# Attention and SwiGLU on one core: batches 4 to 7 with the key decay folded into V and eight heads scored in one run

## The chip, the cores and the metric

The kernel runs on one core of a Trainium2 chip. The metric is the device time in microseconds of one execution. The kernel before took 363.72 us, the median of three runs (363.65 to 364.18).

Engines are named as in the profile: PE (TensorE matmul), PEld (its weight load), DVE (VectorE), ACT (ScalarE), POOL (GpSimd), SP (SyncE, used here as a DMA queue).

## The reference

Eight batches of eight heads, 576 positions, 64 dimensions a head. Causal attention with a decay: `cum` is the running sum of max(s, 0) along the sequence, and a score gets `cum[key] - cum[query]` added before the softmax. The 4608 rows of 512 then go through RMS norm and a SwiGLU layer with 1536 hidden units.

```
scores = scale * q @ k^T                     # scale = 1/8
bias   = -(cum[query] - cum[key])
scores = where(causal, -1e9, scores + min(bias, 0))
attn   = exp(scores - max) ; attn /= sum(attn) + 1e-9
x      = attn @ v                            # [8*576, 512]
xn     = x / sqrt(mean(x*x) + 1e-6) * rms_g
out    = (silu(xn @ w_gate) * (xn @ w_val)) @ w_out
```

The factor exp(-cum[query]) is the same for all keys of a query, so it falls out in the division. What stays is exp(cum[key]), a factor of each key and head. It can be added inside the exponential as a bias of each partition (keys lie on partitions there), or be multiplied into the rows of V and into a column of ones beside V, which gives the sum for the division.

## The kernel before, in words

**Tiles.** A batch's 576 positions are five blocks: four of 128 and a half block of 64. Scores are made transposed, keys on partitions and queries along the free dimension. A step of scores (`s_step`) takes one key block `kb` and half of the heads (`g`), and scores that block's queries and the next block's (256 columns) for four heads. Two heads share PE, one on rows 0 to 63 and one on rows 64 to 127 (`par`), and write to two PSUM banks (`psS`). The half block's step takes all eight heads with 64 columns each. That makes nine steps a batch. Queries further than the next block are not scored: the decay makes them negligible, and a flag worked out on the chip leads to a general path if that does not hold.

ACT takes the exponential head by head, with the head's column of `biasK` as the bias (L302); POOL sets the part above the diagonal to zero (L311). The result lies in one of eight slots of the buffer `E`. An AV step (`av_step`, L344 and L350) multiplies E by V for one query block and four heads: eight matmuls of 65 columns, four for the first block. Its result lies in the bank `psAV` for the first half of the heads and in `psT` for the second. DVE takes the reciprocal of the 65th column (L357) and scales (L359). When both halves are there, ACT sums the squares (L366), POOL works out the norm's factor alpha (L379, L382), DVE scales the row (L389), and a transposing DMA on SP (L400) puts it into `xnT`, a ring of four chunks.

**The FFN.** 512 rows are a chunk; there are nine. `ffn(c)` loops over twelve hidden blocks: four matmuls for the gate (L758), ACT's tanh (L761), four for the value (L767), and DVE's two products U (L770) and Ht (L763). Four row blocks of the output follow, twelve matmuls each (L780), with ACT's copy to `osb` (L785). Gate, value and output take PSUM banks from a ring of four, `psF`.

**The order of the work.** All is written out in one order for each engine when the kernel is built. `step()` is called after every four FFN matmuls: a slot, 36 in a chunk. In each slot a small planner puts in what is ready: pending exponentials and masks, the scale step, loads and casts from side lists (`act_side`, `v_side`, `pool_side`), and in `place()` a score step, an AV step or a transpose. `can_s` and `can_av` hold the rules: so many slots after the inputs were issued, so many since the last step of the kind, and a free slot in E. Score steps come every four slots, nine in 36. `need(c)` puts filler matmuls on PE if a chunk begins before its rows of `xnT` are due; there are none at the starts of chunks now.

**Loads.** For batches 4 to 7, K goes from DRAM to bf16 on the POOL queue (`load_k`), Q comes as fp32 into a raw buffer `kq32` and is cast by POOL (`cast_x`), and both are turned by transposing DMAs on SP (L182). V goes on the POOL queue (`load_v`, L186) into one of two buffers once the AV steps of two batches earlier are done.

## Time and profile before

| | us |
|---|---|
| median of three runs | 363.72 |
| profiled execution, by its span (the page gives no other time of it) | 362.1 |
| PE busy | 346.3 (96%) |
| DVE busy | 275.1 (76%) |
| ACT busy | 240.6 (66%) |
| POOL busy | 174.9 (48%) |
| chunk 0 of the FFN begins, by PE's first gate matmul | 26.5 |
| chunks 3, 4, 5, 6 begin (attention of batches 4 to 7 beside them) | 144.9, 182.6, 220.2, 257.2 |
| chunks 7, 8 begin | 293.3, 324.4 |

The profile is of one execution. In the timeline a row has its start, its length, engine, line, operation and tiles; several equal instructions in a row are merged and counted. PE's lengths overlap, so the distance between starts tells the pace. In the groups by line, "busy, mean ns" comes after the count, then the engine's idle time just before the group and what ended it.

### The profile page before, as it was taken

What the parts mean: (1) busy time and instruction counts of PE and PEld (TensorE: products, weight loads), DVE (VectorE), ACT (ScalarE), POOL (GpSimd) and SP (SyncE); (2) the same over time, 40 slices, a digit from 0 to 9 for tenths busy, and PEclk for the clock granted to TensorE, in tenths of its full rate; (3) what the DMA queues carried; (4) which work ended last, traced back from release to release, by engine and by line L of the source; (5) the groups of instructions that cost most, each with busy time, mean ns of one, the idle gap of its engine ahead of it and who ended that gap; (6) DMA issues with size and microseconds to landing.
All of it is one profiled execution on the core that took longest, in us unless ns stands there. A gap on an engine that the chain in (4) does not pass through costs nothing. (4 is left out here: it accounts for less than half of the span.)

```text
span 362.1 us, 6942 instructions
## 1 busy us (share of the span) xinstructions
PE 346.3 (96%) x2342; PEld 160.6 (44%) x2387; DVE 275.1 (76%) x524; ACT 240.6 (66%) x619; POOL 174.9 (48%) x281
## 2 busy tenths in 40 slices
PE   5889999999999999999999999999999999999993
PEld 2445444543444444444444444444444444444441
DVE  6697988698998889788897988884588558817820
ACT  3988885778787877867778767776777553233311
POOL 6959763738875566979648734622232200000000
PEclk9999999999999999999999999999999999999998
DMA  7999999999999299999999954943200130020011
GB/s 222 144 238 251 173 173 259 170 205 199 172 166 123 31 217 115 181 186 142 184 220 138 128 123 107 128 62 90 71 15 17 60 94 1 0 89 29 1 61 61
DMA packets 124800, 45.68 MB, mean 126 GB/s; under 512 B 103924, under 2 KB 119800, under 8 KB 124760
## 3 DMA queue, kind: packets, MB, share of 16 engines
q0 software_dynamic: 62368, 13.11, 47.6%
q1 hardware_dynamic: 51328, 23.67, 32.5%
q10 hardware_dynamic: 11064, 8.41, 9.5%
q8 instruction: 19, 0.31, 0.4%
q14 instruction: 21, 0.17, 0.2%
HBM read 37.90 MB, written 9.44 MB: 131 GB/s over the span
## 5 line engine op out<-in xcount | busy, mean ns | idle before, releaser
L302 ACT ACTIVATE E<-psS,biasK 128x256 bf16<-128x256 f32 (+3 forms) x328 | 107.3, 413 | 20.5 <-PE psS L278 19.2
L767 PE MATMUL psF<-xnT,wv_sb 128*128 128x512 bf16 x414 | 109.6, 379 | 1.0
L758 PE MATMUL psF<-xnT,wg_sb 128*128 128x512 bf16 x420 | 109.7, 380 | 0.7 <-ACT xnT L416 0.3
L780 PE MATMUL psF<-wout_sb,Ht 128*128 128x512 bf16 x420 | 100.6, 379 | 0.6
L770 DVE SCALAR_TENSOR_TENSOR U<-T,psF 128x512 bf16<-128x512 f32 x108 | 73.7, 682 | 25.5 <-ACT T L761 25.3
L761 ACT ACTIVATE T<-psF 128x512 f32<-128x512 f32 x108 | 64.4, 596 | 41.4 <-PE psF L758 37.5
L311 POOL TENSOR_SCALAR_AFFINE_SELECT E<-E 128x512 bf16<-128x512 bf16 x64 | 45.2, 706 | 84.1 <-ACT E L302 84.1
L763 DVE TENSOR_TENSOR Ht<-U,psF 128x512 bf16<-128x512 bf16 x99 | 67.8, 684 | 7.0
L758 PEld LDWEIGHTS <-wg_sb 128*128 128x128 bf16 x432 | 38.6, 98 | 44.5 <-issue 5.8
L780 PEld LDWEIGHTS <-Ht 128*128 128x128 bf16 x432 | 38.8, 98 | 42.6 <-issue 2.3
L767 PEld LDWEIGHTS <-wv_sb 128*128 128x128 bf16 x432 | 38.5, 98 | 42.2 <-issue 4.0
L785 ACT ACTIVATE osb<-psF 128x512 f32<-128x512 f32 x36 | 21.6, 599 | 33.1 <-PE psF L780 27.6
L389 DVE SCALAR_TENSOR_TENSOR xs_sb<-x_sb,al_all,g_row 128x512 bf16<-128x512 bf16 (+1 forms) x36 | 29.5, 819 | 13.1 <-POOL al_all L382 12.3
L186 POOL DMA_DIRECT2D v_sb<-in_v_dram x40 | 34.8, 872 | 0.0
L366 ACT ACTIVATE xs_sb<-x_sb 128x512 bf16<-128x512 bf16 (+1 forms) x37 | 23.6, 637 | 12.1 <-DVE x_sb L359 11.6
L278 PE MATMUL psS<-kqT 64*128 64x256 bf16 (+2 forms) x304 | 25.9, 256 | 1.6 <-ACT E L302 0.6
L427 DVE TENSOR_TENSOR acc<-acc,mag 128x1280 bf16<-128x1280 bf16 x32 | 27.2, 871 | 0.2
L350 PEld LDWEIGHTS <-E 128*128 128x128 bf16 x320 | 21.7, 98 | 10.1 <-issue 0.2
L382 POOL TENSOR_TENSOR al_all<-al_all,mhalf 128x1 f32<-128x1 f32 (+2 forms) x39 | 22.9, 586 | 3.2
L344 PEld LDWEIGHTS <-E 128*128 128x128 bf16 x256 | 20.0, 98 | 7.7 <-DVE x_sb L359 0.6
L278 PEld LDWEIGHTS <-kqT 64*128 64x128 bf16 x320 | 9.0, 94 | 31.1 <-issue 28.4
L379 POOL TENSOR_SCALAR al_all<-ss_all 128x1 f32<-128x1 f32 (+2 forms) x39 | 9.9, 253 | 25.5 <-ACT xs_sb L366 17.3
(124 smaller groups left out, 301.5 us busy)
## 6 DMA issues: line engine op xcount, KB each, us to landing
out_dram<-osb SPq DMA_DIRECT2D x36, 256.0 KB, 2.3
kq<-in_q_dram ACTq DMA_DIRECT2D x5, 1024.0 KB, 7.8
v_sb<-in_v_dram POOLq DMA_DIRECT2D x32, 128.0 KB, 6.3
kq<-in_k_dram SPq DMA_DIRECT2D x4, 512.0 KB, 5.6
kq<-in_q_dram SPq DMA_DIRECT2D x4, 512.0 KB, 7.5
kq<-in_k_dram ACTq DMA_DIRECT2D x2, 1024.0 KB, 8.8
kqn<-in_k_dram POOLq DMA_DIRECT2D x16, 128.0 KB, 5.6
wout_sb<-in_moe_w_out_dram POOLq DMA_DIRECT2D x2, 768.0 KB, 10.0
```

What stands on the lines that cost most here:

```text
L186: nc.gpsimd.dma_start(out=v_sb[0:n, b % 2, c, :, 0:64], in_=v[b, :, c * 128:c * 128 + n, :].rearrange("h p d -> p h d"))
L278: nc.tensor.matmul(pair[par][:, j * W:j * W + M], lhsT=kT, rhs=qT, start=(j == 0 and not premask), stop=(j == nj - 1))
L302: nc.scalar.activation(out=eo, in_=ei, func=AF.Exp, scale=0.125, bias=biasK[:, kb, bh:bh + 1])
L311: nc.gpsimd.affine_select(out=Ev[:, :, 0:nq], in_=Ev[:, :, 0:nq], pattern=[[0, nh], [1, nq]], compare_op=ALU.is_ge, fill=0.0, base=0, chan ...
L389: nc.vector.scalar_tensor_tensor(out=xs_sb[0:n, (b * NSC + qb) % NX, :], in0=x_sb[0:n, (b * NSC + qb) % NX, :], scalar=al_all[0:n, col:col ...
L427: nc.vector.tensor_tensor(out=acc[:, sl], in0=acc[:, sl], in1=mag[:, sl], op=ALU.max)
L758: nc.tensor.matmul(Gp, lhsT=wg_sb[:, cc, fs], rhs=xnT[:, cc, x0:x0 + DM], start=(cc == 0), stop=(cc == CC - 1))
L761: nc.scalar.activation(out=T, in_=Gp, func=AF.Tanh, scale=0.5)
L763: nc.vector.tensor_tensor(out=Ht[:, fb - 1, :], in0=pend[0], in1=pend[1], op=ALU.mult)
L767: nc.tensor.matmul(Vp, lhsT=wv_sb[:, cc, fs], rhs=xnT[:, cc, x0:x0 + DM], start=(cc == 0), stop=(cc == CC - 1))
L770: nc.vector.scalar_tensor_tensor(out=U, in0=T, scalar=1.0, in1=Gp, op0=ALU.add, op1=ALU.mult)
L780: nc.tensor.matmul(Op, lhsT=Ht[:, fb, tb * 128:(tb + 1) * 128], rhs=wout_sb[:, fb, :], start=(fb == 0), stop=(fb == FB - 1))
```

## The change

Batches 0 to 3 stay. For batches 4 to 7:

- **One run a key block.** `s_run` scores all eight heads at once, into four banks: one from the ring `psF` and `psT` for the second half of the heads, both `psS` banks for the first. Eight matmuls of 256 columns.
- **The half block in the fourth's columns.** The run of block 3 is joined: each head has 128 columns of block 3's own queries, 64 tail queries against block 3's keys, and the same 64 against the half block's keys, in one 256-column field. 24 matmuls. Four runs a batch, not nine steps. In E the half block's scores lie at columns 192 to 255, and the last AV step reads 128 columns from 64 and from 128, so that its 64 rows come out on partitions 64 to 127; the steps behind it work on these (`part_of`).
- **The decay.** `vwx` = exp(biasK) for these batches, once, in chunk 0. `fold_b` on POOL multiplies V's block by it and copies it into the 65th column; an AV step waits for its block's fold.
- **The exponential.** One activation of 512 columns for a bank, without bias: four a run, one in each of the next four slots (`exp_q`).
- **Order.** Runs at least nine slots apart (`PERIOD`). AV steps of these batches use `psAV` for both halves, at least two slots apart. The squares come one slot later and the scale step four slots after its AV.
- **Loads.** Q of these batches alternates between the two raw buffers and is loaded a batch earlier; K and V loads on POOL are two slots apart (`PACE`).

```diff
+    MB = 4
+    PERIOD, PACE = 9, 2
+    vwx = mp.tile([128, NSC, (B - MB) * H], FP32, name="vwx")
+    def raw(b, w):
+        return (b + 1) % 2 if b >= KB else w
...
+    def s_run(b, kb):
+        p, join = b % 2, kb == 3
+        N = 192 if join else 256
+        fb, tt, ps = psF(), psT32(), psS()
+        banks = {1: (fb, tt), 0: (ps[:, 0, :], ps[:, 1, :])}
+        es = {g: take_slot((b, kb, g), 3 if join else 2) for g in (1, 0)}
+        if join:
+            eslot.update({(b, 4, g): es[g] for g in es})
+        def keys(rs, c, hp):
+            return kqTx[rs, p, 0, c, hp, :] if b >= KB else kqTn[rs, p, 0, hp, c * 128:c * 128 + 128]
+        for g in (1, 0):
+            for j in (0, 1):
+                hp = 2 * g + j
+                parts = [(kb, kqTx[:, p, 1, kb:kb + 2, hp, :], 0, 256)]
+                if join:
+                    tail = kqTx[:, p, 1, 4, hp, 0:64].rearrange("d (p r) -> d r p", r=4)
+                    parts = [(3, kqTx[:, p, 1, 3, hp, :].rearrange("d (r p) -> d r p", r=4), 0, 32),
+                             (3, tail, 32, 16), (4, tail, 48, 16)]
+                for i, (c, qT, o, n) in enumerate(parts):
+                    for par in (0, 1):
+                        rs = slice(par * 64, par * 64 + 64)
+                        to = banks[g][par][:, j * 256:j * 256 + 256]
+                        if join:
+                            to = to.rearrange("k (r p) -> k r p", r=4)[:, :, o:o + n]
+                        nc.tensor.matmul(to, lhsT=keys(rs, c, hp), rhs=qT[rs],
+                                         start=(j == 0 and i == 0), stop=(j == 1 and i == len(parts) - 1))
+        def exps(g, par):
+            to = E[:, es[g], 2 * par:2 * par + 2, :]
+            src = banks[g][par]
...
+            nc.scalar.activation(out=to, in_=src, func=AF.Exp, scale=0.125)
+        def mask(g, c, q0, nq):
+            Ev = E[:, es[g], :, q0:q0 + nq]
+            nc.gpsimd.affine_select(
+                out=Ev, in_=Ev, pattern=[[0, 4], [1, nq]], compare_op=ALU.is_ge, fill=0.0, base=0,
+                channel_multiplier=-1)
+            done["S", b, c, g] = slot[0]
+        def part(g, par):
+            exps(g, par)
...
+            if par:
+                pending.append(lambda: mask(g, kb, 0, 128))
+                if join:
+                    pending.append(lambda: mask(g, 4, 192, 64))
...
+        exp_q.extend((join, lambda a=(g, par): part(*a)) for g in (1, 0) for par in (0, 1))
+    def fold_b(b, c):
+        i = (b - MB) * H
+        nc.gpsimd.tensor_tensor(
+            out=v_sb[:, b % 2, c, :, 0:64], in0=v_sb[:, b % 2, c, :, 0:64],
+            in1=vwx[:, c, i:i + H].unsqueeze(2).to_broadcast([128, H, 64]), op=ALU.mult)
+        nc.gpsimd.tensor_copy(out=v_sb[:, b % 2, c, :, 64], in_=vwx[:, c, i:i + H])
+        done["W", b, c] = slot[0]
...
-            ps = psT32() if b > 0 and g == 1 else psAV()
+            ps = psT32() if 0 < b < MB and g == 1 else psAV()
...
+            e, back, own = j, 128, 0
+            if b >= MB:
+                e = 2 * (j % 2) + j // 2
+                if qb == 4:
+                    back, own = 64, 128
...
+        if b >= MB:
+            if slot[0] - last["S"] < 3 or slot[0] - last["run"] < PERIOD or slot[0] - max(last[x] for x in ("AVT", "TT")) < 2:
+                return False
+            return run_ready()
...
-        if b > 1 and not ready(8, "V", b):
+        if b > 1 and not ready(8, "V", b) or b >= MB and not ready(3, "W", b, qb):
...
+        for _ in range(1):
+            if exp_q:
+                exp_q.pop(0)[1]()
...
-            if ready(5 if (b, qb) == (1, 1) else 3, "AV", b, qb, 1):
+            if ready(5 if (b, qb) == (1, 1) else 4 if b >= MB else 3, "AV", b, qb, 1):
...
-            run_side(pool_side)
+            if not run_side(pool_side) and fold_seq and ready(9, "V", *fold_seq[0]):
+                fold_b(*fold_seq.pop(0))
...
+        put(act_side, 30, lambda: nc.scalar.activation(out=vwx, in_=biasK[:, :, MB * H:BH], func=AF.Exp))
```

More of the change, by code (lines that the diff above doesn't have):

```diff
@@ L240, in take_slot, with slot_free @@
         return sl
-    def slot_free():
-        return eread.get(ecount[0] % NE, 0) == 0
+    def slot_free(n=1):
+        return all(eread.get((ecount[0] + i) % NE, 0) == 0 for i in range(n))
     def masks(pair):
@@ L448 @@
     x_seq = []
+    fold_seq = [(b, c) for b in range(MB, B) for c in range(NSC)]
     def at(*key):
@@ L490, in main @@
             last["L"] = slot[0]
+            last["P"] = slot[0] + 2
         def tail():
@@ L504, in key @@
             load_k(b, c)
+            last["P"] = slot[0]
             done["K", b, c] = slot[0]
@@ L524, in casts @@
         if b >= KB:
-            pool_side.extend((lambda: free(0) and slot[0] % 2 == 0, lambda c=c: key(c)) for c in range(NSC))
+            pool_side.extend((lambda: free(0) and slot[0] - last["P"] >= PACE, lambda c=c: key(c)) for c in range(NSC))
         fns = [(1, lambda r=r: cast_x(nc.gpsimd, b, 1, r)) for r in range(NSC)]
@@ L557, in after_av, with val @@
                 return
-            early(v_side, 11 if b == 1 else 6, [lambda r=r: load_v(b + 2, r) for r in range(NSC)]
+            def val(r):
+                load_v(b + 2, r)
+                last["P"] = done["V", b + 2, r] = slot[0]
+            n = len(v_side)
+            early(v_side, 11 if b == 1 else 6, [lambda r=r: val(r) for r in range(NSC)]
                   + [lambda: done.__setitem__(("V", b + 2), slot[0])])
+            if b > 1:
+                v_side[n:] = [(lambda c=c: c() and slot[0] - last["P"] >= PACE, f) for c, f in v_side[n:]]
     def in_av(b, hp):
@@ L583, in do_s @@
         b, kb, g = key
+        last["S"] = done["R", b, kb] = slot[0]
+        if b >= MB:
+            last["run"] = done["R", b, 4] = slot[0]
+            return s_run(b, kb)
         second = s_step(b, kb, g, pair, masked)
@@ L587, in do_s @@
             done["S", b, 4, 1] = slot[0]
-        last["S"] = slot[0]
         return second
@@ L648, in can_av @@
         b, qb, g = av_seq[0]
+        if g and b < MB and slot[0] - last["RT"] < 1:
+            return False
         if slot[0] - last["AV"] < (1 if (b, qb) == (1, 3) else 2):
@@ L681, in warm, with step @@
             nc.tensor.matmul(ps, lhsT=ident_bf, rhs=mneg, start=True, stop=True)
-    def step(bare=False):
+    def step(bare=False, tanh=False):
         slot[0] += 1
```

108 lines of the change are left out of this document (72 added, 36 removed).

## The prediction

> **What bounds the kernel now.** I read the page's first part, then a table by stretches, the waits, and last the order of time on PE.
>
> ```profile
> span 362.1 us, 6942 instructions
> PE 346.3 (96%) x2342; PEld 160.6 (44%) x2387; DVE 275.1 (76%) x524; ACT 240.6 (66%) x619; POOL 174.9 (48%) x281
> ```
>
> PE is hardly ever without work, but its busy time is modelled, so this does not yet say that PE is the limit. The table cuts the span where chunks 3 to 7 of the FFN begin (columns: length, then busy time and instructions of PE, its weight loader, DVE, ACT and POOL, granted clock, DMA share, GB/s). The attention of batches 4 to 7 lies in the first four rows; the fifth row is almost bare FFN.
>
> ```profile
> 144.90:182.60 37.70, 37.44 (x265) 16.82 (x268) 32.12 (x58) 28.18 (x79) 29.88 (x47) 1.00 1.58 176
> 182.60:220.20 37.60, 37.34 (x266) 17.05 (x270) 33.77 (x67) 28.98 (x80) 22.51 (x37) 1.00 1.25 148
> 220.20:257.20 37.00, 36.73 (x252) 16.59 (x256) 25.75 (x51) 27.06 (x74) 14.16 (x25) 1.00 0.64 91
> 257.20:293.30 36.10, 35.84 (x241) 16.45 (x245) 24.31 (x48) 24.28 (x66) 9.28 (x18) 1.00 0.16 47
> 293.30:324.40 31.10, 30.94 (x143) 14.09 (x145) 20.68 (x35) 11.11 (x22) 0.00 (x0) 1.00 0.10 37
> ```
>
> A bare chunk takes 31.1 us, 144 matmuls at 0.216; the others take 5.0 to 6.6 more, at a granted clock of 1.00 throughout. What fills that is seen in PE's own order (start, length, line, how many):
>
> ```profile
> 200.37 1.02 PE L767 MATMUL psF<-xnT,wv_sb 128*128 128x512 bf16 x4
> 201.32 0.39 PE L278 MATMUL psS<-kqT 64*128 64x256 bf16 x4
> 201.65 1.04 PE L758 MATMUL psF<-xnT,wg_sb 128*128 128x512 bf16 x4
> ...
> 202.77 1.03 PE L767 MATMUL psF<-xnT,wv_sb 128*128 128x512 bf16 x4
> 203.63 1.03 PE L758 MATMUL psF<-xnT,wg_sb 128*128 128x512 bf16 x4
> 204.49 1.03 PE L767 MATMUL psF<-xnT,wv_sb 128*128 128x512 bf16 x4
> ...
> 208.62 1.03 PE L780 MATMUL psF<-wout_sb,Ht 128*128 128x512 bf16 x4
> 209.58 0.29 PE L278 MATMUL psS<-kqT 64*128 64x64 bf16 x8
> 209.80 0.39 PE L780 MATMUL psF<-wout_sb,Ht 128*128 128x512 bf16 x1
> ```
>
> A slot of four FFN matmuls takes 203.63 - 202.77 = 0.86. A score step between two slots costs 201.65 - 200.37 - 0.86 = 0.42, an AV step 202.77 - 201.65 - 0.86 = 0.26, the half block's score step 209.80 - 208.62 - 0.86 = 0.32. A batch is eight score steps, one half step and ten AV steps (two of them half as long): 3.4 + 0.3 + 2.3 = 6.0, spread over 36 slots of a chunk. With 31.1 that is 37.1, against 37.6 and 37.0 in the second and third rows. There is hardly room for stalls: PE's own list of instructions sets the time, and what leaves that list is won.
>
> **The score groups (the gain).** Four heads in a step are two pairs, a pair sharing PE's two halves of 64 rows. If a pair of 256 columns takes half of what 512 take, 0.1075, two pairs make 0.21 of the 0.42, and the four pairs of 64 columns in the half step make 0.11 of the 0.32. Both leave 0.21, with two pairs and with four: a fixed price for going into a group of 64-row matmuls and out of it. The waits show the way in: the weight loader stood idle 0.42 on average (28.4 in 67 times) before the first small load, and nothing that the profile shows released it:
>
> ```profile
> PEld L278 <- issue: 28.4, 67, 0.6
> L278 PE MATMUL psS<-kqT 64*128 64x256 bf16 x128 | 12.5, 274 | 0.0
> L278 PE MATMUL psS<-kqT 64*128 64x64 bf16 x32 | 1.2, 192 | 0.0
> ```
>
> The counts are those of batches 4 to 7: 128 / 4 = 32 steps and 32 / 8 = 4 half steps, together 32 x 0.42 + 4 x 0.32 = 14.7 us. After the change a run has all eight heads: four pairs, 0.43 + 0.21 = 0.64. The joined run (fourth block and half block) has, for each pair of heads, 128 + 64 + 64 columns instead of 256: the same 0.43, in twelve pairs. Sixteen runs make 10.2 us. **Gain 4.5 us**; the streamed columns are the same, and twenty of 36 entries at 0.21 go (4.2, and 0.3 for garbage columns no longer computed).
>
> The joined run reads its tail queries with a stride of four elements and writes each head's scores in strips of 16 and 32 columns. No row has either. Nearest is the 64-column row above (0.027 a pair), which I take: nothing. The other end is that such a pair runs at the 256-column price: 32 pairs of 64 by 0.08 and 16 of 128 by 0.054, 3.4 us. A gain is excluded, since fewer columns do not stream.
> The Trainium skill's page "SBUF — State Buffer", section "Door 1: The DMA port swizzle", says that matmuls slow down significantly on any non-contiguous PSUM access, lines there being 8 bytes, and that SBUF reads keep their rate up to four bf16 apart; by the first, the sum would lie toward the other end, a gain near 1.1, and no run here shows it yet.
>
> **The exponentials (nothing).** Old and new shapes, from the stretch of these batches and, for 512 columns without bias, from batch 0:
>
> ```profile
> L302 ACT ACTIVATE E<-psS,biasK 128x256 bf16<-128x256 f32 x96 | 38.9, 473 | 7.1 <-PE psS L278 6.3 <-POOL al_all L379 0.9
> L302 ACT ACTIVATE E<-psS,biasK 128x64 bf16<-128x64 f32 x63 | 17.8, 325 | 6.1 <-PE psS L278 6.1
> L302 ACT ACTIVATE E<-psS,biasK 128x128 bf16<-128x128 f32 x32 | 12.1, 379 | 3.7 <-PE psS L278 3.7
> L318 ACT ACTIVATE E<-psS 128x512 bf16<-128x512 f32 x6 | 3.3, 595 | 0.4 <-PE psS L278 0.2
> ```
>
> These 68.8 us become 16 x 4 x 0.6 = 38.4. ACT was idle 8.6 to 11.8 us in each of the four rows and PE's steps above add up without waits for it, so 30 us less on ACT move the end by nothing; they make T and the squares a little earlier. The one exponential of the decay in chunk 0 (160 columns, under 0.47) falls into that idle time too.
>
> **The fold on POOL (nothing, hidden, but tight at first).**
>
> ```profile
> L333 POOL TENSOR_TENSOR v_sb<-v_sb,vw 128x520 bf16<-128x520 bf16 x5 | 5.2, 1068 | 0.0
> ```
>
> Twenty folds at 1.07 and twenty copies of eight columns are 26 us; no row has such a copy, its ends are the fold's own 1.07 and DVE's 0.18 for four columns (203.56, below), and I take 0.25, near the latter for its size. Masks are eight of 512 elements a batch and two smaller, in place of nine. POOL idles 7.8, 15.1, 22.8 and 26.8 us in the four rows, and gets 6.6 a batch. In the first of them that leaves about one microsecond free. If the cover is gone, the masks and alpha (L379, L382) behind a fold come up to 1.3 us later, and DVE's scale step with them.
>
> **Banks.** A run takes one of the four psF banks, the psT bank and both psS banks. The psF bank shortens the ring by one slot (0.86) while the run itself puts in 0.64, so the FFN's margin falls by 0.22. The gate bank filled from 201.65 was free at 204.80 (U, below); with a run in front, its fourth successor would have started 204.49 + 0.64 = 205.13. Between 0 and 16 x 0.22 = 3.5; I take 0.3. Both AV halves now use psAV, two slots apart, instead of psAV and psT:
>
> ```profile
> 203.56 0.18 DVE L357 RECIPROCAL rZ<-psT 128x4 f32<-128x4 f32 x1
> 203.77 0.42 DVE L359 TENSOR_TENSOR x_sb<-psT,rZ 128x256 bf16<-128x256 f32 x1
> 204.12 0.68 DVE L770 SCALAR_TENSOR_TENSOR U<-T,psF 128x512 bf16<-128x512 f32 x1
> ...
> 172.27 0.19 PE L350 MATMUL psAV<-v_sb,E 128*128 128x65 bf16 x1
> 171.76 1.71 POOL L156 CAST kqn<-kq 128x512 bf16<-128x512 f32 x3
> 172.79 1.24 DVE L389 SCALAR_TENSOR_TENSOR xs_sb<-x_sb,al_all,g_row 128x512 bf16<-128x512 bf16 x1
> 173.94 1.25 DVE L421 TENSOR_SCALAR mag<-kqn 128x2560 uint16<-128x2560 uint16 x1
> 175.32 0.42 DVE L359 TENSOR_TENSOR x_sb<-psAV,rZ 128x256 bf16<-128x256 f32 x1
> ```
>
> An AV step's bank is free when DVE has scaled it: at 204.19 for the step that ended before 202.77, and a second one two slots later would start at 204.49, so the usual margin is 0.3. The later rows show a bad case: a scale step and a check stood ahead in DVE's order, the bank came free at 175.74, and two slots after 172.30 are 174.02: a wait of 1.7. In the new order the scale step comes four slots after the second half, and the next pair seven after it, so it is out of the way of most pairs; checks remain. Between 0 and 20 x 1.7 = 34, with the usual case, which is nearest, at 0; I take 0.2.
>
> **Order and loads (nothing).** No run begins before batch 3 has been scored:
>
> ```profile
> 144.56 0.39 PE L278 MATMUL psS<-kqT 64*128 64x256 bf16 x4
> 182.61 0.39 PE L758 MATMUL psF<-xnT,wg_sb 128*128 128x512 bf16 x1
> xnT<-xs_sb SPq DMA_TRANSPOSE x35, 3.7
> ```
>
> The first row is batch 4's first score step now, at the end of slot 107. A run every nine slots is the same pace, 36 slots a batch. The tightest use is chunk 4 (slot 144, the second row), which needs batch 4's second block: run in slot 117, its second AV half twelve slots later in 129, scale step in 133, transpose landing 3.7 us on, near 139. Five slots to spare; chunk 5 has as many. If the cover is gone, three filler matmuls stand in each slot of delay, 0.65. The second raw buffer, the wider spacing of K, V and Q loads and the later AV of batch 4 move loads within this slack and put nothing on PE. The squares come one slot later and the scale step four slots after its AV, instead of three, so their distance is the same. On SP the same transposes go out; V of batch 6 is loaded from six slots behind batch 4's last AV (151), so from 157 to about 165, folded nine slots later and read from 190 on.
>
> **Sum.** The profiled execution is 362.1 long by its span; the median of the runs is 363.72, so 1.6 lies around the span, and I keep that. 362.1 - 4.5 + 0.3 + 0.2 = 358.1, with 1.6 around it **359.7**, a gain of 1.1%.
>
> **The rivals.**
> *Joined run slow* (strided reads, strips): 4.5 - 3.4 leaves 1.1 less the bank waits of 0.5: 363.1 at worst, about 362 in the middle. For it: no row shows such an access. Against it: the half step's 64-column pairs, already narrow, cost no more than their columns.
> *POOL and DVE late.* A fold ahead of alpha makes the scale step wait, DVE then frees T's and U's banks late, and PE waits in the FFN. For it: the first stretch leaves POOL one microsecond, and DVE 5.6 and 3.8 in the first two rows; a scale step took 1.24 at 172.79 with casts on POOL beside it (171.76 to 173.47), against 0.75 as a rule:
>
> ```profile
> L389 DVE SCALAR_TENSOR_TENSOR xs_sb<-x_sb,al_all,g_row x36: 732/750/1235, 41.9 to 293.2; 128x512 bf16<-128x512 bf16 x28, 64x512 bf16<-64x512 bf16 x8
> ```
>
> Against it: the later rows have 11 us free on DVE, and ACT's load falls by a quarter. If each of the first ten folds costs DVE 0.5 and half of that reaches PE, 2.5: 362; with all twenty in full, 10 us, slower than now. The point from which the whole gain is gone is 0.2 us of PE for each fold.
> The Trainium skill's page "SBUF — State Buffer", section "Who interferes with whom", calls the port pair of DVE and GpSimd an exclusive lock held for a whole instruction; by that rule the long scale step is a lock and each fold another chance for one. The trace agrees with 1.235 against 0.750, without naming the cause.
> *One AV bank (slower).* At each of 20 pairs PE's second AV half waits for DVE's scaling of the first. It decides from 0.2 us a pair; at a fifth of the pairs like 172.3 and the rest 0.1 late it costs 4 x 1.7 + 16 x 0.1 = 8.4: 367.6. For it: the usual margin is 0.3. Against it: DVE's order between two halves holds no scale step in most pairs.
> *The price is not per group.* If each pair paid its own 0.105 (half of 0.21), a run of four pairs would cost 0.84 and the joined one, with twelve, 1.69: 4 x (3 x 0.84 + 1.69) = 16.8 against 14.7, so 2.1 slower, and 366.3 with the bank terms. Against it: the half step has four pairs and pays 0.21 once.
>
> **How the numbers follow.** Forecast 0.57 (its own range 358.9 to 360.8: bank terms from 0, less 0.3 for rounding, to 1.6); joined run slow 0.09 (0.08 faster, 0.01 same); POOL and DVE late 0.19 (361 to 364.5: 0.13 faster, 0.03 same, 0.03 slower); one bank 0.12; price not per group 0.03. 0.2% of this kernel, 0.7 us, is about what a measurement can tell from no change. Faster: 0.57 + 0.08 + 0.13 = 0.78; same 0.01 + 0.03 = 0.04; slower 0.03 + 0.12 + 0.03 = 0.18. From 358.9 to 363.2 the range holds the forecast, the joined run and most of the late POOL, about 0.79. Cases of both signs are in play, so the likeliest one's own range stands above.
>
> **What would show it.** Right: PE's order of time has sixteen groups of scores, each 0.64 more than a slot, the joined ones too; the wait "issue" before the small weight loads falls by some twenty times; the four chunks fall from 37.7, 37.6, 37.0 and 36.1 by 1.1 each, moved a little between them. Exponentials of 512 elements at 0.6 and POOL at 90% or more in the first of the four stretches. Wrong: joined groups of 0.8 and more; PE idle before AV matmuls, released by DVE's L359; PE waiting for U or Ht; DVE waiting for alpha much longer than now; filler matmuls at the start of chunk 4 or 5.

## The result, and the profile after

The changed kernel takes 374.2 us (median of four runs, 373.16 to 376.22) against 363.95 for the kernel before beside it: 1.0275 of its time, with a 95% interval of 1.0232 to 1.0317. The forecast was 359.7, with a range up to 363.2. The change is slower, by about 10 us. Ratios here and below come from undisturbed executions of both kernels, so they need not be the quotient of the medians.

The page of the changed kernel, first part:

```profile
span 373.1 us, 6871 instructions
PE 346.8 (93%) x2374; PEld 165.4 (44%) x2419; DVE 290.7 (78%) x524; ACT 215.0 (58%) x492; POOL 208.6 (56%) x325
```

PE is as busy as before (346.8 against 346.3) in a span that is 11.0 longer: PE now stands still. ACT fell from 240.6 to 215.0. DVE rose from 275.1 to 290.7 with the same 524 instructions. It got no new work, so its instructions have become longer; this is the first line of the page that says what happened.

The table by stretches of the changed kernel: chunks 2 to 5, then two short pieces of them (length; busy time and instructions of PE, its weight loader, DVE, ACT, POOL; granted clock; DMA share; GB/s). A row over its chunks 2 to 7 follows.

```profile
106.40:148.20 41.80, 38.73 (x280) 17.86 (x283) 36.62 (x62) 29.64 (x81) 26.82 (x38) 0.99 1.10 154
148.20:190.50 42.30, 38.40 (x244) 17.84 (x248) 34.56 (x52) 20.14 (x41) 34.94 (x52) 0.93 1.05 122
190.50:229.10 38.60, 36.00 (x261) 17.57 (x264) 32.79 (x54) 20.47 (x43) 30.54 (x48) 1.00 1.01 118
229.10:267.00 37.90, 36.20 (x262) 17.57 (x266) 32.71 (x56) 20.50 (x43) 28.52 (x44) 1.00 0.87 93
147.60:151.00 3.40, 3.18 (x13) 1.23 (x11) 2.21 (x4) 1.86 (x5) 2.71 (x4) 0.50 0.91 227
161.30:164.70 3.40, 3.40 (x10) 1.22 (x8) 1.89 (x3) 1.26 (x3) 0.63 (x2) 0.50 1.04 105
...
106.40:335.50 229.10, 216.81 (x1465) 103.25 (x1492) 185.29 (x316) 123.13 (x272) 132.64 (x203) 0.99 0.78 102
```

The same chunks of the kernel before:

```profile
106.51:324.40 217.89, 216.32 (x1434) 98.57 (x1461) 170.05 (x316) 149.24 (x400) 99.40 (x159) 1.00 0.84 107
```

Chunks 3 to 5 took 37.7, 37.6 and 37.0 before and take 42.3, 38.6 and 37.9. Chunk 2, in whose last slot batch 4's first run now stands, went from 38.4 to 41.8. So the loss is mostly at the start of the changed batches. In two pieces of 3.4 us the granted clock is 0.50: work of 1.7 us takes 3.4 there (in the second, a slot of four FFN matmuls takes 1.71, from 161.49 to 163.20, where 0.86 is usual). The profile of the kernel before shows no such piece.

What PE waited for, chunks 2 to 7 of the changed kernel (engine, tile and line; then who released it: us in total, times, longest):

```profile
PE psAV L430 <- DVE x_sb L446: 3.7, 3, 2.1
PE psT L366 <- DVE x_sb L446: 2.7, 1, 2.7
PE psF L899 <- DVE U L902: 2.5, 4, 2.0
PE psAV L436 <- POOL E L383: 0.7, 1, 0.7
```

That is 9.6 us in nine waits, nearly all for a PSUM bank that DVE reads out late. The reason stands ahead of these reads in DVE's order. The timeline of the changed kernel at three of the waits (start, length, engine, line, tiles, count; in brackets the wait before the row and its releaser), with a clean run of scores between them:

```profile
140.47 2.38 DVE L508 TENSOR_SCALAR mag<-kqn 128x2560 uint16<-128x2560 uint16 x1
...
142.23 1.52 POOL L402 TENSOR_TENSOR v_sb<-v_sb,vwx 128x512 bf16<-128x512 bf16 x1
...
143.32 2.30 DVE L514 TENSOR_TENSOR acc<-acc,mag 128x1280 bf16<-128x1280 bf16 x2
145.65 1.16 DVE L508 TENSOR_SCALAR mag<-kqn 128x2560 uint16<-128x2560 uint16 x1
...
146.93 0.42 DVE L446 TENSOR_TENSOR x_sb<-psT,rZ 128x256 bf16<-128x256 f32 x1
...
147.41 0.28 PE L366 MATMUL psT<-kqT 64*128 64x256 bf16 x1 [2.71 <-DVE x_sb L446]
...
157.16 2.73 DVE L476 SCALAR_TENSOR_TENSOR xs_sb<-x_sb,al_all,g_row 64x512 bf16<-64x512 bf16 x1
158.15 2.20 POOL L163 CAST kqn<-kq 128x512 bf16<-128x512 f32 x3
160.53 1.17 PE L899 MATMUL psF<-xnT,wv_sb 128*128 128x512 bf16 x3 [1.97 <-DVE U L902]
...
207.30 1.03 PE L899 MATMUL psF<-xnT,wv_sb 128*128 128x512 bf16 x4
208.26 0.28 PE L366 MATMUL psF<-kqT 64*128 64x256 bf16 x1
...
208.80 1.04 PE L890 MATMUL psF<-xnT,wg_sb 128*128 128x512 bf16 x3
...
216.67 3.17 DVE L508 TENSOR_SCALAR mag<-kqn 128x2560 uint16<-128x2560 uint16 x1
219.24 1.49 POOL L402 TENSOR_TENSOR v_sb<-v_sb,vwx 128x512 bf16<-128x512 bf16 x1
219.88 2.55 DVE L514 TENSOR_TENSOR acc<-acc,mag 128x1280 bf16<-128x1280 bf16 x2
...
222.55 0.42 DVE L446 TENSOR_TENSOR x_sb<-psAV,rZ 128x256 bf16<-128x256 f32 x1
223.03 0.20 PE L430 MATMUL psAV<-v_sb,E 128*128 128x65 bf16 x1 [2.07 <-DVE x_sb L446]
```

At 216.67 the first pass of a check takes 3.17 us, and the two passes behind it 2.55. (A check is DVE's search for the largest magnitude in K or Q, which the flag needs: one pass makes `mag`, two take the maximum into `acc`.) POOL's folds run beside them (one at 219.24; 1.49 long). The read of `psAV` stands behind all that, at 222.55, and PE waits 2.07 for it. The same happens before the first run, at 147.41, for `psT`, with a fold at 142.23. At 157.16 it is the scale step, 2.73 where 0.75 is usual, with three POOL casts in a row beside most of it; U comes late and PE waits 1.97.

PE's own list did become shorter as forecast: a clean run costs 208.80 - 207.30 - 0.86 = 0.64, of which 0.54 lie behind its first matmul.

### The profile page after: what moved, and what is told of

Same layout as the page of the kernel before. It is cut to its first block, busy times and chain, and to the rows that moved or that the text cites. A ratio compares the mean times of both kernels' runs of the same rounds, so it can differ in the third digit from the quotient of the medians.

```text
span 373.1 us, 6871 instructions
## 1 busy us (share of the span) xinstructions
PE 346.8 (93%) x2374; PEld 165.4 (44%) x2419; DVE 290.7 (78%) x524; ACT 215.0 (58%) x492; POOL 208.6 (56%) x325
## 5 line engine op out<-in xcount | busy, mean ns | idle before, releaser
L899 PE MATMUL psF<-xnT,wv_sb 128*128 128x512 bf16 x422 | 111.4, 383 | 3.4 <-DVE U L902 2.5
L890 PE MATMUL psF<-xnT,wg_sb 128*128 128x512 bf16 x415 | 111.7, 384 | 1.1 <-ACT xnT L503 0.3
L912 PE MATMUL psF<-wout_sb,Ht 128*128 128x512 bf16 x417 | 97.8, 379 | 0.7
L890 PEld LDWEIGHTS <-wg_sb 128*128 128x128 bf16 x432 | 39.7, 98 | 45.2 <-issue 5.5
L917 ACT ACTIVATE osb<-psF 128x512 f32<-128x512 f32 x36 | 21.6, 599 | 50.8 <-PE psF L912 38.4
L309 ACT ACTIVATE E<-psS,biasK 128x256 bf16<-128x256 f32 (+3 forms) x136 | 44.7, 420 | 3.5 <-PE psS L285 3.3
L476 DVE SCALAR_TENSOR_TENSOR xs_sb<-x_sb,al_all,g_row 128x512 bf16<-128x512 bf16 (+1 forms) x36 | 32.8, 911 | 10.5 <-POOL al_all L469 10.4
L383 POOL TENSOR_SCALAR_AFFINE_SELECT E<-E 128x512 bf16<-128x512 bf16 (+1 forms) x40 | 27.9, 706 | 22.2 <-ACT E L379 12.4
L318 POOL TENSOR_SCALAR_AFFINE_SELECT E<-E 128x512 bf16<-128x512 bf16 x28 | 19.8, 708 | 24.8 <-ACT E L309 24.6
L514 DVE TENSOR_TENSOR acc<-acc,mag 128x1280 bf16<-128x1280 bf16 x32 | 32.2, 1033 | 0.2
L446 DVE TENSOR_TENSOR x_sb<-psAV,rZ 128x256 bf16<-128x256 f32 (+1 forms) x61 | 25.9, 424 | 2.1
```

The lines of the kernel that those rows point to most:

```text
L309: nc.scalar.activation(out=eo, in_=ei, func=AF.Exp, scale=0.125, bias=biasK[:, kb, bh:bh + 1])
L383: nc.gpsimd.affine_select(out=Ev, in_=Ev, pattern=[[0, 4], [1, nq]], compare_op=ALU.is_ge, fill=0.0, base=0, channel_multiplier=-1)
L446: nc.vector.tensor_tensor(out=xo[:, g * 256:(g + 1) * 256].rearrange("p (h d) -> p h d", h=4), in0=pv[R, :, 0:64], in1=rZ[R].unsqueeze(2). ...
L476: nc.vector.scalar_tensor_tensor(out=xs_sb[R, (b * NSC + qb) % NX, :], in0=x_sb[R, (b * NSC + qb) % NX, :], scalar=al_all[R, col:col + 1], ...
L514: nc.vector.tensor_tensor(out=acc[:, sl], in0=acc[:, sl], in1=mag[:, sl], op=ALU.max)
L890: nc.tensor.matmul(Gp, lhsT=wg_sb[:, cc, fs], rhs=xnT[:, cc, x0:x0 + DM], start=(cc == 0), stop=(cc == CC - 1))
```

## The experiments

Two theories stood at the start. The first, A in the texts below: DVE's checks and scale steps and POOL's instructions (folds, copies, casts) stretch each other when they overlap; banks are then released late. Its rival: the new order of banks is itself too tight (one `psAV`, a run on `psF` and `psT`), and PE would wait whatever POOL does.

**No folds.** This kernel leaves out the decay of batches 4 to 7.

```diff
     def fold_b(b, c):
-        i = (b - MB) * H
-        nc.gpsimd.tensor_tensor(... in1=vwx ..., op=ALU.mult)
-        nc.gpsimd.tensor_copy(out=v_sb[:, b % 2, c, :, 64], in_=vwx[:, c, i:i + H])
         done["W", b, c] = slot[0]
```

> The folds and copies on POOL are left out for batches 4 to 7 (their output then lacks the decay); the order of everything else is the same. Theory A (DVE's checks and POOL's folds hold each other up, so that the shared banks of PSUM come free late): the checks between 179 and 262 us go back from 1.7 - 3.2 us to about 1.0, the waits of PE for psAV there (1.6, 2.5, 0.8, 0.9) shrink to under 0.3 each, the wait of 2.7 us before the first run (147.4) shrinks below 1.5 and its stretch at half clock goes; the wait of 2.0 at 160.5 stays, since casts stand beside that scale step and not folds. 374 becomes 364 to 367. Theory B (one AV bank is too few whatever POOL does): the psAV waits keep over half of their 5.8 us, 370 to 372.

**No checks.** The flag then covers batches 0 to 2 only.

```diff
         dve_side.extend((lambda w=w: when(w), f) for w in (ws if b < KB else (0, 1)) for f in (
-            lambda w=w: check_mag(b, w), lambda: check_max(0), lambda: check_max(1),
+            *((lambda: None,) * 3 if b >= 3 else
+              (lambda w=w: check_mag(b, w), lambda: check_max(0), lambda: check_max(1))),
```

> The magnitude checks of batches 3 to 7 on DVE are left out (the flag then covers batches 0 to 2 only). Theory A: the long DVE instructions in front of the AV scaling are gone, so the psAV waits behind the joined runs (1.6, 2.5, 0.8) and the wait before the first run go, with its half clock; the wait behind alpha (0.9 at 231) and the one for U at 160.5 stay. 363 to 367. Theory B (folds keep POOL late, masks and alpha with them): DVE's checks do not matter, 371 or more.

Without folds 364.78 us, 1.0017 of before (0.9997 to 1.0037); without checks 363.51, 0.9998 (0.9977 to 1.0019). Each gives back about 10 us. Neither removed work from PE, and both took it from an engine with idle time. The groups by line between 135 and 300 (count, then busy us and mean ns), first of the kernel before:

```profile
L427 DVE TENSOR_TENSOR acc<-acc,mag 128x1280 bf16<-128x1280 bf16 x18 | 14.6, 841 | 0.1
L421 DVE TENSOR_SCALAR mag<-kqn 128x2560 uint16<-128x2560 uint16 x9 | 8.8, 977 | 0.1
```

of the changed kernel:

```profile
L514 DVE TENSOR_TENSOR acc<-acc,mag 128x1280 bf16<-128x1280 bf16 x18 | 19.6, 1128 | 0.1
L508 DVE TENSOR_SCALAR mag<-kqn 128x2560 uint16<-128x2560 uint16 x9 | 14.9, 1656 | 0.0
L402 POOL TENSOR_TENSOR v_sb<-v_sb,vwx 128x512 bf16<-128x512 bf16 x20 | 24.5, 1224 | 0.1
L405 POOL CAST v_sb<-vwx 128x8 bf16<-128x8 f32 x20 | 9.0, 452 | 0.0
```

without folds:

```profile
L509 DVE TENSOR_TENSOR acc<-acc,mag 128x1280 bf16<-128x1280 bf16 x18 | 14.4, 843 | 0.1
L503 DVE TENSOR_SCALAR mag<-kqn 128x2560 uint16<-128x2560 uint16 x9 | 7.7, 857 | 0.0
```

and without checks:

```profile
L402 POOL TENSOR_TENSOR v_sb<-v_sb,vwx 128x512 bf16<-128x512 bf16 x20 | 21.3, 1063 | 0.1
L405 POOL CAST v_sb<-vwx 128x8 bf16<-128x8 f32 x20 | 4.8, 240 | 0.0
```

The same instructions of the same shape: a check's first pass takes 857 ns in the kernel without folds and 1656 with them, an eight-column copy 240 without checks and 452 with them. Either partner taken away restores the other. These are means of all such instructions; in the changed kernel eleven of the twenty folds lie beside a check's pass. Which of POOL's two instructions, the product or the copy, does more was not separated. PE's waits in chunks 2 to 7 fall from 9.6 to about 2.5, nearly all of the one kind that has nothing to do with folds (without checks 2.4 for U and 0.3 for a mask). Without folds:

```profile
PE psF L894 <- DVE U L897: 2.5, 4, 2.0
```

The waits for `psAV` and `psT` are gone though the bank order is the same, and neither kernel has a piece at half clock in its profiled execution. So the rival falls, as far as these two banks go.

**Two banks for an AV pair.** The run takes two banks from the ring and leaves `psT` to the second AV half.

```diff
-        fb, tt, ps = psF(), psT32(), psS()
+        fb, tt, ps = psF(), psF(), psS()
...
-            ps = psT32() if 0 < b < MB and g == 1 else psAV()
+            ps = psT32() if b > 0 and g == 1 else psAV()
```

> A run takes two psF banks instead of one psF and psT, and the second AV half goes to psT again. Theory A: PE no longer waits for psAV or psT, as the bank has four slots or more; the checks stay long. The ring of psF is one bank shorter around a run, so waits for U and Ht may grow: 0 to 0.5 a run. 374 becomes 364 to 370. Theory B (PE waits because DVE is late, and will wait for any bank): the psAV waits turn into psF waits of the same size, 372 to 376.

It takes 380.05, 1.0453 of before (1.0426 to 1.0481): slower still, and past what I had set down. The waits of that kernel, chunks 2 to 7:

```profile
PE psF L366 <- DVE U L902: 4.3, 4, 2.5
PE psAV L436 <- POOL E L383: 3.6, 2, 2.9
PE psF L899 <- ACT osb L917: 2.6, 1, 2.6
```

The wait for `psAV` behind a late scaling is gone. In its place PE waits for the ring, of which a run now takes two banks: each batch's second run takes 1.57 to 3.53 from its first matmul to the next FFN matmul, where 0.54 is usual. It also waits 3.6 for masks on POOL and 2.6 for an output copy on ACT. So another bank only moves the waits here. These rows come to about as much as the 9.6 before, and why the kernel is slower still was not followed to the end. I had taken the first cause, and the gain of a second bank, for separable; with a ring of four they are not.

**Strips left out.** Each part of the joined run writes contiguous PSUM columns. Scores then lie at other queries' places; this kernel leaves out the right order of the scores.

```diff
-                            to = to.rearrange("k (r p) -> k r p", r=4)[:, :, o:o + n]
+                            to = banks[g][par][:, j * 256 + 4 * o:j * 256 + 4 * (o + n)]
+                            to = to.rearrange("k (r p) -> k r p", r=4)
```

> In the joined runs each part is written as one contiguous piece of the bank instead of strips of 16 or 32 columns (the scores of these runs then stand at the wrong queries). The joined run costs 1.11 where 0.64 was forecast. If the strips in PSUM are the cause: 0.64, four times 0.47 less, 372. If the reading of the tail queries with a stride of four is the cause: unchanged, 374.

**Tail queries read contiguously.** Here too the scores of the tail lie at other queries' places.

```diff
-                    tail = kqTx[:, p, 1, 4, hp, 0:64].rearrange("d (p r) -> d r p", r=4)
+                    tail = kqTx[:, p, 1, 4, hp, 0:64].rearrange("d (r p) -> d r p", r=4)
```

> In the joined runs the tail queries are read one after the other, not four apart (the tail's scores of these runs then stand at permuted queries); all else as after the change. If the stride costs: pairs of 64 columns go at 0.03 instead of 0.036 to 0.06, the joined run falls from 0.89 to 0.64, and the time by 1.0, to 373. If the short pairs cost that much however they are read (twelve weight loads): 0.89 and 374.

Times: 374.04 (1.029, 1.0255 to 1.0324) and 375.72 (1.0304, 1.0264 to 1.0343). Neither is a gain; the group itself is what to look at. PE's timeline in the changed kernel, from the first matmul of a joined run to the next FFN matmul:

```profile
217.16 0.23 PE L366 MATMUL psF<-kqT 64*128 64x128 bf16 x1
...
217.96 0.82 PE L912 MATMUL psF<-wout_sb,Ht 128*128 128x512 bf16 x3
```

with the strips left out:

```profile
215.64 0.23 PE L367 MATMUL psF<-kqT 64*128 64x128 bf16 x1
...
216.44 1.04 PE L913 MATMUL psF<-wout_sb,Ht 128*128 128x512 bf16 x4
```

and with the tail read contiguously:

```profile
217.81 0.23 PE L366 MATMUL psF<-kqT 64*128 64x128 bf16 x1
...
218.37 0.82 PE L912 MATMUL psF<-wout_sb,Ht 128*128 128x512 bf16 x3
```

0.80, 0.80 and 0.56, and the other three joined runs of each kernel are the same within 0.01. Writing in strips costs nothing; reading the moving operand with a stride of four bf16 elements costs 0.24 a run, 1.0 us for the four. (Counted from the end of the slot before, as the 0.64 is, the joined run of the changed kernel costs 0.90; no row gives the 1.11 of the expectation above.) The time cannot show this 1.0: in the second kernel's profiled execution a third piece at half clock, 223.7 to 227.1, follows its wait for `psAV`, which costs 1.7, and executions of one kernel differ by as much (mean granted clock 0.981 to 0.994 in its four, 0.986 to 0.994 in those of the changed kernel).

**Casts of Q on ACT.** From the batches on whose K comes as bf16 (`KB`).

```diff
-        fns = [(1, lambda r=r: cast_x(nc.gpsimd, b, 1, r)) for r in range(NSC)]
+        fns = [(1, lambda r=r: cast_x(nc.gpsimd if b < KB else nc.scalar, b, 1, r)) for r in range(NSC)]
```

> The casts of Q for batches 4 to 7 run on ACT instead of POOL, in the same slots. Theory A (a POOL instruction next to a DVE instruction with two inputs in SBUF stretches it): the scale step of 2.73 us at 157 us falls to 0.75 - 1.3, the wait for U of 2.0 us goes and its half clock of 3.4 us with it: 374 to 370 - 371; the wait before the first run and those for psAV stay. Rival (the scale step is long by itself, with 64 partitions): 2.7 us and 374.

**Folds only outside the checks' phase.** Checks stand at slot 25 and later of each chunk.

```diff
-            if not run_side(pool_side) and fold_seq and ready(9, "V", *fold_seq[0]):
+            if not run_side(pool_side) and fold_seq and phase() < 24 and ready(9, "V", *fold_seq[0]):
```

> POOL's folds are put only into the first 24 slots of a chunk, the checks of DVE lie in the other twelve; nothing is left out. Theory A: as without folds, 363 to 366: checks of 0.8 to 1.1 us, no wait for psAV over 0.3, the wait of 2.0 for U stays. Theory B (POOL's load as such, wherever it stands): 370 or more, and DVE's scale steps, U and Ht wait in the first 24 slots instead.

Casts on ACT: 372.66, 1.0179 (1.0149 to 1.021). Folds moved: 366.94, 1.006 (1.0038 to 1.0082). The scale step, min/median/max in ns, in the changed kernel:

```profile
L476 DVE SCALAR_TENSOR_TENSOR xs_sb<-x_sb,al_all,g_row x36: 736/752/2727, 41.8 to 314.1; 128x512 bf16<-128x512 bf16 x28, 64x512 bf16<-64x512 bf16 x8
```

with the casts on ACT:

```profile
L476 DVE SCALAR_TENSOR_TENSOR xs_sb<-x_sb,al_all,g_row x36: 734/751/1177, 42.6 to 313.7; 128x512 bf16<-128x512 bf16 x28, 64x512 bf16<-64x512 bf16 x8
```

and with the casts on POOL and the folds moved:

```profile
L476 DVE SCALAR_TENSOR_TENSOR xs_sb<-x_sb,al_all,g_row x36: 734/751/3672, 41.8 to 306.4; 128x512 bf16<-128x512 bf16 x28, 64x512 bf16<-64x512 bf16 x8
```

So the third kind of wait, for U, comes from POOL's casts beside a scale step: without them the longest step is 1.18 and the 2.0 us wait is gone. The other waits stay, and the time falls little: in the profiled execution a second piece at half clock follows the wait for `psAV` at 221.90, where the changed kernel had none. With the folds moved, the `psAV` waits are gone and a check's first pass is 959 ns, but a scale step meets casts (and loads of V and K on POOL ahead of them) and takes 3.67, and PE waits for U. The longest of that kernel's waits in chunks 1 to 8:

```profile
PE psF L899 <- DVE U L902: 4.4, 4, 3.1
```

Each edit mends its own wait and leaves the other.

**All mends together.** Casts on ACT, folds outside the checks' phase, and the joined run with contiguous tail queries in and out (two exponentials of 256 a bank put the columns right, so that nothing is left out).

```diff
-                to = to.rearrange("k j (p r) -> k j p r", r=4)
-                src = src.rearrange("k (j r p) -> k j p r", j=2, r=4)
+                src = src.rearrange("k (j n) -> k j n", j=2)
+                nc.scalar.activation(out=to[:, :, 128:256], in_=src[:, :, 128:256], func=AF.Exp, scale=0.125)
+                to = to[:, :, 0:128].rearrange("k j (p r) -> k j p r", r=4)
+                src = src[:, :, 0:128].rearrange("k j (r p) -> k j p r", r=4)
```

> Folds outside the checks, Q casts on ACT, and the joined run with contiguous reads and writes (two exponentials of 256 elements a bank in place of one of 512); the full computation. If the three causes add up: PE's list as forecast, sixteen runs at 0.64, no wait over 0.3: 359.5 to 361, 0.989 to 0.992 of the time before. If a new wait takes their place (ACT, with the casts and four more exponentials a batch): 362 to 364.

362.99, 0.9966 (0.9953 to 0.9979): faster than before, with 2.2 us of waits for U left. Two further edits on top of it, each alone: the scale step of a batch's fourth query block three slots after its AV instead of four, and batch 4's casts on POOL as they were.

```diff
-            if ready(5 if (b, qb) == (1, 1) else 4 if b >= MB else 3, "AV", b, qb, 1):
+            if ready(5 if (b, qb) == (1, 1) else 4 if b >= MB and qb != 3 else 3, "AV", b, qb, 1):
```

> As the run with all three mendings, and the scale step of a batch's fourth block one slot earlier, so that it no longer shares a slot with an AV scaling two slots before a run. If that crowd on DVE makes U late and PE wait for the psF bank (0.6, 0.6 and 1.0 at the batches' second runs): these waits fall below 0.3 and the time by 1.5, to 361.5. If the scale step then waits for alpha instead: unchanged, 363.

```diff
-        fns = [(1, lambda r=r: cast_x(nc.gpsimd if b < KB else nc.scalar, b, 1, r)) for r in range(NSC)]
+        fns = [(1, lambda r=r: cast_x(nc.gpsimd if b <= KB else nc.scalar, b, 1, r)) for r in range(NSC)]
```

> As the run with all three mendings, but batch 4's Q casts stay on POOL; only those of batches 5 to 7 go to ACT. If batch 4's casts, which fall beside batch 3's head by head exponentials, hold ACT up (a score step waited 0.6 for psS near 122 us): the stretch from 106 us falls from 39.2 to 38.6 and the time to 362.4. If not: 363.

361.88, 0.9945 (0.9928 to 0.9961), and 362.44, 0.9957 (0.9942 to 0.9971). Both intervals overlap that of all mends, so neither small gain is clear by its time alone; in the trace of the first the waits for U fall from 2.2 to 0.9 us.

**The groups without the fold.** The runs, but with the bias in each head's own exponential as before (eight slots a run, not four), and no fold; with contiguous reads and writes in the joined run. Nothing is left out. The second has batch 4's casts on POOL and those of 5 to 7 on ACT.

```diff
-        def exps(g, par):
+        def exps(g, par, j):
...
+                nc.scalar.activation(out=eo, in_=ei, func=AF.Exp, scale=0.125,
+                                     bias=biasK[:, c, b * H + h:b * H + h + 1])
...
-        exp_q.extend((join, lambda a=(g, par): part(*a)) for g in (1, 0) for par in (0, 1))
+        exp_q.extend((join, lambda a=(g, par, j): part(*a)) for g in (1, 0) for par in (0, 1) for j in (0, 1))
```

> One part alone: runs of eight heads, joined half block (contiguous), but the decay stays in the exponentials, head by head, one head in each of eight slots; V isn't folded, Q casts on POOL. If the groups make the gain and the fold on POOL and the wide exponentials only bring the waits: 360.5 to 362.5, checks at 1.0, no wait for psAV over 0.3, the wait of 2.0 at the scale step beside casts stays. If ACT at its old load makes T late beside the longer runs: 363 or more.

> The same with the Q casts of batches 5 to 7 on ACT. If the wait beside the casts is the only one left: 1.5 to 2.5 less than with the casts on POOL, 359 to 360.5. If ACT is then too full (its load as before, and three us a batch more): no better than with casts on POOL, waits of PE for U behind a late T.

365.72, 1.0057 (1.0035 to 1.008), and 366.99, 1.008 (1.0064 to 1.0096). Both are a little slower than the kernel before. PE's longest waits in the first, chunks 1 to 8:

```profile
PE psS L367 <- ACT E L380: 2.9, 6, 1.0
```

With narrow exponentials in eight slots the `psS` banks are still full when the next run comes, nine slots on. With the casts on ACT as well, the same waits grow to 4.4 us in seven times. So the fold seems to have a use beyond the bias: it makes the wide exponential possible, and that empties the banks in time. This holds only for that pace of the exponentials; two narrow ones a slot were not tried, and these waits are less than half of what the kernel is behind the bare list below.

**Both further edits.** On top of all mends:

> All mendings together, the full computation: folds outside the checks, Q casts of batches 5 to 7 on ACT, contiguous joined run, the scale step of the fourth block a slot earlier. If the two small ones add: 361.9 less 0.65, 361.2, a ratio of 0.992 to 0.994.

361.15 (360.3 to 361.28), 0.9913 of before (0.9897 to 0.993): the best version that computes everything, 2.6 us faster than before and 13 faster than the change as made. Its waits for U are down to 0.9.

**The bare list.** The last kernel without folds and without the checks of batches 3 to 7:

```diff
     def fold_b(b, c):
-        ...
         done["W", b, c] = slot[0]
...
+            *((lambda: None,) * 3 if b >= 3 else
...
-            if not run_side(pool_side) and fold_seq and phase() < 24 and ready(9, "V", *fold_seq[0]):
+            if not run_side(pool_side) and fold_seq and ready(9, "V", *fold_seq[0]):
```

> The same without folds (batches 4 to 7 lack the decay) and without the magnitude checks of batches 3 to 7. If PE's list is worth the 4.5 us that single steps gave, and only DVE's lateness takes from it: 359.2 to 360.2. If the list is worth less: 361 or more, with no wait of PE over 0.3 to be seen.

359.36 (359.19 to 359.96), 0.9877 (0.9859 to 0.9894). This is PE's list nearly without waits. Its chunks 2 to 7, and its one wait for U in chunks 1 to 8:

```profile
106.87:321.00 214.13, 213.65 (x1493) 101.71 (x1492) 147.97 (x287) 131.15 (x303) 87.59 (x148) 1.00 0.80 109
```

```profile
PE psF L898 <- DVE U L901: 0.3, 1, 0.3
```

Against this row the changed kernel's 229.10 is 15.0 longer. Counted pieces: waits 9.6 - 0.3, half clock 2 x 1.7, joined runs 1.0; together 13.7. Of the remaining 1.3, three shorter waits that the list above leaves out (0.3, 0.2 and 0.2) make 0.7; the rest was not followed.

## Why the prediction was wrong

**The score groups: right, within 0.7.** 0.64 a run, and 0.66 for the joined one when it reads contiguously: the fixed price of 0.21 is paid once for a group. In chunks 2 to 7, where all sixteen runs lie, the bare list is 3.8 us shorter than the kernel before (214.13 against 217.89), with 0.3 of waiting left in it; the term was 4.5. The whole time differs by 4.4 (363.74 - 359.36), which is nearer partly by luck, since the rest of it lies outside those chunks. The price for each pair, the fourth rival, is excluded.

**The exponentials: right.** Wide ones take 0.59; in chunks 2 to 7 of the changed kernel PE waits nowhere for ACT.

**The joined run: mis-sized.** Taken as nothing, with 3.4 as the other end; measured 4 x 0.24 = 1.0. I had put strided reads and strips under one bound. Only the reads cost. The row that was nearest (64 columns, 0.027 a pair) was contiguous on both sides and could not tell.
The Trainium skill's page "SBUF — State Buffer", section "Door 1: The DMA port swizzle", has it the other way about: non-contiguous PSUM slows matmuls, and reads from SBUF keep their rate as long as two of them fall into one line of 16 bytes, as they do four bf16 apart (eight apart is the page's own figure). Strips of 16 and 32 columns cost nothing here (0.80 with and without them), and a stride of four bf16 cost 0.24 of 0.80; the measurement decides.

**The fold on POOL, "nothing, hidden": this is the step that failed.** POOL had time for it. But a fold is not hidden by POOL's idle time alone: with the folds DVE's check pass goes from 0.86 to 1.66 on average, with single ones at 2.38 and 3.17, and PE waits for the banks that DVE reads behind it. Leaving the folds out, or only moving them away from the checks, takes those waits away. I looked for the cost in what waits for POOL (masks and alpha) and not in what DVE executes at the same time, though the scale step of 1.235 at 172.79 was quoted as evidence. The rival *POOL and DVE late* had the right pair of engines, and its price with all folds in full, 10 us, is near the 9.4 that leaving them out gave back. That is luck: the price was the 0.5 of one scale step for each of twenty folds, while the loss came in a few waits of 0.4 to 2.7 behind stretched checks and in the half clock behind such waits. Its mechanism, alpha late behind a fold, did not come: DVE waited 9.1 us for alpha in chunks 2 to 7, and 11.1 before. One wait of 0.7 (at 230.90) is for a mask on POOL; the stretched checks explain those for `psAV` and `psT`, a scale step beside casts that for U. It got a chance of 0.19, with 0.03 of that slower. Of the prediction's own signs of being wrong, three came: joined groups of 0.8 and more, PE idle before AV matmuls behind the scaling, and PE waiting for U.
The Trainium skill's page "SBUF — State Buffer", section "Who interferes with whom", says that a DVE instruction with two SBUF inputs, or in a two-port mode, and a GpSimd instruction that reads SBUF exclude each other for a whole instruction, and that the order of issue decides who waits. The trace agrees: the pair lengthens on both sides (1656 and 452 ns against 857 and 240), and either one alone does not. That one holds the other off for a whole instruction, and that the check's first pass with its one input runs in such a mode, these means do not show. The prediction cited this rule and weighed it by the 0.5 us of one scale step; a check is longer, its three instructions stand close together, and eleven of the twenty folds met them.

**Banks: the second step that failed, as a consequence.** `psAV` was put at 0.2 and measured 3.7, with 2.7 more for `psT`, which had no term. The bad case was in the text (a check ahead of the scaling, 1.7), and then set aside because the scale step moves out of the way, with the words "checks remain". They did: the period of 36 slots is that of the checks too, and the AV pair after the joined run fell into them in three of the four batches (waits of 1.23, 2.07 and 0.43; beside batch 7's there is no check). Bank order alone is not the cause: without folds, or without checks, these waits vanish with the same banks, and with two banks they only move. So the rival *One AV bank* had the place and not the reason (its 367.6 also leaves out the ring's 0.3). The ring was put at 0.3; it gave 2.5, of which 2.0 is one scale step among casts and the rest three waits of 0.17, about the term. The 2.0 belongs to what I had under "Order and loads (nothing)": the scale step meets the casts with and without the folds. That the new distance between AV, scale step and casts brought them together is likely, but no run put the old distance back.

**The clock: not considered.** 3.4 us of the loss is two pieces at half clock behind waits. No term had it: in the kernel before PE waits 0.6 us at most once it has begun, and its profile shows no piece at half clock.

**The point named as decisive** was 0.2 us of PE for each fold. Undoing the folds moved the time by about 9.4 us (374.2 to 364.78), 0.47 a fold, the half clock included.

## What to carry to other kernels

Work put on an engine with idle time is hidden only if it does not lengthen what runs beside it on another engine. On DVE and POOL look for the longest instructions of the other engine that will overlap it, and for what is queued behind those. When a bank is to be freed by an engine that also runs long side work, compare the periods of both: if they are equal, the worst case comes back in every period. And when all waits come to a few microseconds at a time, count the clock behind them as well.

## What the hardware showed that was not expected

- **Half clock behind a wait.** Waits of 2.0 to 3.1 us in the middle of dense work were followed, in several kernels, by 3.4 us at a granted clock of 0.50, worth 1.7 us each. Executions of one kernel show the same step: with the folds moved, five at a mean clock of 0.991 to 0.992 took 366.92 to 367.42, and two at 0.995 and 0.996 took 365.28 and 365.48. Not always: the same wait of 2.0 us for U was followed by one in the changed kernel (161.3) and by none in the profiled executions without folds, without checks or with the strips left out. The Trainium skill's page "TensorE: Matmul & The Clock Gate", section "What's actually happening", gives a gate of four in eight pulses after an idle window of 3.4 us that runs freely. The length and the 0.50 agree; the waits here are shorter than that window, and what decides between the two outcomes was not tried.
- **DVE and POOL stretch each other**, the more so when several of POOL's instructions lie beside one of DVE's: a check's pass of 0.86 took 3.17, a scale step of 0.75 took 2.73 and 3.67 with casts in a row beside it (1.18 at most with the casts on ACT), and an eight-column copy of 0.24 took 0.8 at worst.
- **A stride of four bf16 in the moving operand** takes the joined run from 0.56 to 0.80, while writing in PSUM strips of 16 and 32 columns leaves it unchanged, whether the reads are strided (0.80 with and without strips) or not (0.56 both ways).
